# Probability rows of 64 bytes, earlier transposes for the second unit, and the last scatter behind the conditional slots

## The chip, the cores and the metric

The kernel runs on one core of a Trainium2 chip. Its time is the device time of one execution in microseconds. TensorE is called PE here, VectorE DVE, ScalarE ACT, GpSimd Pool, SyncE SP; `SPq` and `POOLq` are instructions of a queue itself (issues of transfers, waits, loads of a register).

## What is computed

Three stages in a row on [4, 576, 512] activations, all in float32. First attention in 8 heads with a causal window of 64. Then a gated feed-forward layer with a convolution of three taps:

```python
h = relu(x @ w_in)
conv = sum(conv_w[k] * hp[:, k:k + S, :] for k in range(3))
y = (h * sigmoid(conv)) @ w_out
```

Then a mixture of 8 experts, in which a token takes its own best expert or holds that of the token before it:

```python
fresh = argmax(logits[b, s])
e = fresh if s == 0 or local_gate[b, s] < 0.5 else prev_e
out[b, s] = p[e] * (relu(y[b, s] @ w1[e]) @ w2[e])     # p = softmax(logits[b, s])
```

## The kernel before

**Layers one and two.** `main(b)` takes the four batches in turn; `attention` of the next batch is woven into the feed-forward products of this one. `ffn_out` (line 478) makes 128 rows of `y` in PSUM with 24 products of 512 columns; ACT moves them into one of two `ysb` buffers (line 499), and SP writes them to `y_dram` (line 500). A row of `y_dram` has 528 columns: 512 of `y` and 16 more, of which column 512 is to hold the token's probability. The last block of 128 rows is made in two halves of 24 products of 256 columns by `ffn_out_last` (lines 503 to 536).

**Routing.** `route_init` (line 729) sets up constants; SP writes zeros into the 16 further columns of `y_dram`, 128 rows at a time (line 789). The gates and the chosen experts follow behind the last batch's products. `chosen` (line 881) ends with the probability of each token in `psel`, 128 partitions x 18, and writes it twice from SP: into `p_dram`, one float for a token (line 888), and into column 512 of `y_dram` (line 889). `slots_of` sorts the tokens by expert into slots and ends with the lists `gidx` (which rows a slot reads, line 992) and `sidx` (which rows it writes), the experts of the slots, and the count of slots `tcnt`.

**Units.** A unit is a slot of 128 tokens of one expert ("S") or a group of two slots and 32 further rows of one expert ("B"). 14 units always run (`NU`): S, then five times B and S, then three S. The rows of a unit are gathered from `y_dram` by Pool (`gather`, line 1146), transposed by PE and split into a high and a low part by ACT and DVE (`X`, line 1168); `take` copies the gathered probability into `pcur`. The first unit is different: most of its rows are gathered before the last block is done (line 1361), those of the last two blocks are added by products with selection matrices within `ffn_out_last` (`x_half`, line 512, after ten products of the second half), and its probabilities are gathered from `p_dram` (line 1366).

`step(t)` (line 1262) is the order of work of one unit, written out by hand: `first_S` or `first_B` makes the hidden layer with the split weights of `w1`, `HT` transposes it, `second_S` or `second_B` multiplies by `w2`. `ahead()` transposes the next unit's rows and starts gathers of later units. `job()` runs a split of weights: a cast on ACT (line 1111) and the remainder on DVE (line 1115). For unit 0, `ahead()` stands behind all 24 products of `second_S`. `second_S` ends with an eviction on ACT that scales by `pcur` (line 1246), and a scatter by Pool to `out` (line 1160). SP loads the weights of later units under a condition (a slot with the same expert needs none).

**Conditional slots.** Behind the 14 units every engine loads the count of slots (line 1420), compares and branches (line 1424). Up to six more slots would run there, each one nested in the condition of the slot before it (`alone`, line 1338); no product of them stands in this trace.

PE, DVE and ACT follow the order of the code (`manual_schedule`); so do Pool and SP in the last stage.

Of the kernel before, what the change touches and what calls it, by code (L numbers as in the profile page):

```python
# [21 lines left out]
def kernel(  # L22
# [14 lines left out]
    nc = tc.nc  # L37
# [20 lines left out]
    dram = ctx.enter_context(tc.tile_pool(name="dram", bufs=1, space=DRAM))  # L58
    DY = DM + 16
    y_dram = dram.tile([N, DY], F32, name="y_dram")  # L60
    p_dram = dram.tile([N, 1], F32, name="p_dram")

    ident = const.tile([P, P], F32, name="ident")
    make_identity(nc, ident)
# [29 lines left out]
    if True:  # L94
# [616 lines left out]
        R0 = 2 * S // P  # L711
        gidx = const.tile([P, NCOL], I32, name="gidx")
        sidx = const.tile([P, NCOL], I32, name="sidx")
        pcur = [const.tile([P, 3], F32, name=f"pcur{i}") for i in range(2)]
        nc.gpsimd.memset(pcur[0], 0.0)
        eslot = const.tile([1, NS + NB], I32, name="eslot")
        tcnt = const.tile([1, 1], I32, name="tcnt")
# [11 lines left out]
        def route_init():  # L729
# [54 lines left out]
            tl("A", [P, NT, P], BF16)  # L784
            tl("aZ", [P, 2, P])
            nc.gpsimd.memset(tl("x0", [P, DY]), 0.0)
            for i in range(NT):
                w = slice(0, DY) if i >= NT - 2 else slice(DM, DY)
                nc.sync.dma_start(out=y_dram[i * P:(i + 1) * P, w], in_=rt["x0"][:, w])
# [91 lines left out]
        def chosen():  # L881

            ex = rt["ex"]
            nc.vector.tensor_tensor(ex, ex, rt["oh"], op=ALU.mult)
            psel = rt["psel"] = r1.tile([P, NT], F32, name="psel")
            nc.vector.tensor_reduce(psel, ex, axis=AX.X, op=ALU.add)
            nc.vector.tensor_tensor(psel, psel, rt["ssum"], op=ALU.mult)
            nc.sync.dma_start(out=p_dram[:, :].rearrange("(i p) o -> p (i o)", p=P), in_=psel)
            nc.sync.dma_start(out=y_dram[:, DM:DM + 1].rearrange("(i p) o -> p (i o)", p=P), in_=psel)

        def slots_of():
# [254 lines left out]
    def gather(t):  # L1146
        for g, (c, _, n) in zip(rows(t), cols(t)):
# [3 lines left out]
                bounds_check=N - 1, oob_is_err=False,  # L1151
            )

    def take(t):

        for j, (g, (_, _, n)) in enumerate(zip(rows(t), cols(t))):
            nc.gpsimd.tensor_copy(pcur[t % 2][0:n, j:j + 1], g[0:n, DM:DM + 1])

    def scatter(c, n, o):
        nc.gpsimd.indirect_dma_start(  # L1160
# [70 lines left out]
            nc.vector.scalar_tensor_tensor(hl[:, f], ps, 0.0, hh[:, f].bitcast(F32), op0=ALU.max, op1=ALU.subtract)  # L1231
            after(f)

    def second_S(t, mids={}):
        hh, hl = (x[:, :, 0:P] for x in hT)
        ps = ps_o.tile([P, DM], F32, tag="o", name="psO")
        n = 0
        for f in range(KF):
            H_, L_ = (w[:, f % 2, :] for w in w2_set[f // 2])
            for a, w in ((hh, H_), (hh, L_), (hl, H_)):  # L1240
                nc.tensor.matmul(ps, a[:, f], w, start=n == 0, stop=n == 3 * KF - 1)  # L1241
                n += 1
                for m in mids.get(n, ()):
                    m()
        c = cols(t)[0][0]
        nc.scalar.activation(o_v[0], ps, AF.Copy, scale=pcur[t % 2][:, 0:1])
        scatter(c, P, o_v[0])

    def second_B(t, after):
        hh, hl = hT  # L1250
# [11 lines left out]
    def step(t, first=(), second=(), late=()):  # L1262

        kind = units[t][0]
        end = t + 1 == NU
        before = t and units[t - 1][0] == "B"
        jobs = list(first)

        def job(n=1):
            for _ in range(n):  # L1270
                if jobs:
                    jobs.pop(0)()

        def ahead():
            if not end:
                X(t + 1)
                n = 4 if t > 2 * NB - 3 else 3
                while coming[0] < min(t + n, NU):
                    gather(coming[0])
                    coming[0] += 1  # L1280

        if kind == "S":
            y = [lambda j=j: Y(t - 1, j) for j in range(3)] if before else [lambda: None] * 3
            job(2)
            first_S(t, {
                (0, 6): (y[0], job), (0, 10): (y[1],),
                (1, 7): (lambda: job(9), lambda: HT(0), *late), (1, 10): (y[2],),
            })
            if t:
                ahead()  # L1290
            jobs.extend(second)
            second_S(t, {3: (lambda: HT(1), lambda: job(9))})
            if not t:
                ahead()
        else:
            first_B(t, lambda f: job())
            job(9)
            ahead()
            jobs.extend(second)
            second_B(t, lambda d: job(2))  # L1300
            job(9)

    def w1_jobs(t):
        if t >= NU:
# [17 lines left out]
    def run():  # L1322
        gather(1)
        load1(1)
        cast(raw2, w2_set, KORD[3])
        for kk in KORD:
            rest_of(raw2, w2_set, kk)
        load2(1)
        for t in range(NU):
            if t == 0:  # L1330
                step(t, (), w1_jobs(1))
            elif units[t][0] == "B":
                step(t, w1_jobs(t + 1) + w2_jobs(t), w1_jobs(t + 2))
            else:
                *w, (c, r) = w2_jobs(t, True)
                step(t, w + [c], w1_jobs(t + 2) if t > 2 * NB - 1 else (), (r,))

    def alone(t):

# [7 lines left out]
        first_S(t)  # L1347
        HT(0)
        HT(1)
        second_S(t)  # L1350

    def tail():
        first = [ffn_out(i, False, 1) for i in (I0, I0 + 1)]
# [5 lines left out]
        for i in range(I0 + 2, NT):  # L1359
            if i == NT - 1:  # L1360
# [3 lines left out]
                    bounds_check=N - 2 * P - 1, oob_is_err=False,  # L1364
                )
                nc.gpsimd.indirect_dma_start(
                    out=pcur[0][:, 0:1], out_offset=None, in_=p_dram[:, :],
                    in_offset=bass.IndirectOffsetOnAxis(ap=gidx[:, 0:1].bitcast(U32), axis=0),
                    bounds_check=N - 1, oob_is_err=False,
                )  # L1370
# [2 lines left out]
    with tc.manual_schedule(engines={mybir.EngineType.PE, mybir.EngineType.DVE, mybir.EngineType.Activation}):  # L1373
# [42 lines left out]
        ps_o = ctx.enter_context(tc.tile_pool(name="ps_o", bufs=2, space=PSUM))  # L1416
        ps_y = ctx.enter_context(tc.tile_pool(name="ps_y", bufs=2, space=PSUM))
        with tc.manual_schedule():
            run()
    slots = nc.values_load(tcnt[0:1, 0:1], min_val=0, max_val=NS)  # L1420

    def others(t):
# [3 lines left out]
                others(t + 1)  # L1426

    others(NU)


# [27 lines left out]
```

## Time and profile before

| | |
|---|---|
| median of 3 runs | 640.96 us (640.54 to 641.39) |
| profiled execution: its time | 641.02 us |
| its span, first to last instruction | 639.0 us |
| mean granted clock of PE | 0.981 of 2.4 GHz |
| busy share of PE, DVE, ACT, Pool | 94%, 66%, 62%, 21% |
| moved by the DMA engines | 92.19 MB, 144 GB/s in the mean |

The profile is one execution. Times in it are microseconds from the start of the span. The chain that ended last is followed back from the last instruction, at each step to what released it. An idle time in brackets stands just before the instruction it belongs to, with what ended it.

### The profile page before, as it was taken

The numbers are of one execution on the slowest core, as the hardware profiler recorded it, in microseconds if no ns is written. First come the engines' busy times: TensorE is split into PE (matmuls) and PEld (weight loads), VectorE is DVE, ScalarE is ACT, GpSimd is POOL, SyncE is SP. The second block draws the span as 40 slices with busy tenths as digits, with TensorE's granted clock in tenths as the row PEclk, the third lists the DMA queues.
The fourth block names the chain that finished last, engine by engine and source line by source line (L and its number), as shares of the span: only waits on it lengthen the run. The fifth ranks groups of instructions, "written<-read, shape, count | busy, mean of one in ns | idle before, by whom it ended". The sixth has DMA issues, their size and how long they took to land.

```text
span 639.0 us, 12841 instructions
## 1 busy us (share of the span) xinstructions
PE 603.3 (94%) x4648; PEld 549.0 (86%) x4648; DVE 420.4 (66%) x972; ACT 394.7 (62%) x926; POOL 134.7 (21%) x198
## 2 busy tenths in 40 slices
PE   6779999999999999999999699999999999999993
PEld 4658998899999999999977688989899899898872
DVE  3888999626883268825868568548556485576860
ACT  3477788646795477934734157657655576567850
POOL 3412000001431023322520122132031320303200
PEclk9889999999999999999999899999999999999997
DMA  7893524442324221118108768858759583433830
GB/s 180 202 244 83 163 66 104 102 122 54 72 61 115 67 54 35 34 36 284 54 1 20 191 226 286 280 185 298 272 174 326 178 269 140 142 91 119 289 135 14
DMA packets 104342, 92.19 MB, mean 144 GB/s; under 512 B 78626, under 2 KB 78898, under 8 KB 104272
## 3 DMA queue, kind: packets, MB, share of 16 engines
q1 hardware_dynamic: 99152, 79.48, 43.5%
q0 software_dynamic: 3488, 10.24, 4.6%
q10 hardware_dynamic: 1632, 1.57, 0.9%
q8 instruction: 39, 0.64, 0.4%
q14 instruction: 31, 0.25, 0.1%
HBM read 89.53 MB, written 10.72 MB: 157 GB/s over the span
## 4 chain that ended last, share of the span: by engine, by line
PE 64%; DVE 12%; DMA 10%; issue 8%; ACT 4%; ACTq 0%; POOLq 0%; POOL 0%; DVEq 0%
PE psO L486 13%; PE psM L444 11%; PE psH L1228 10%; PE psO L1257 8%; PE psO L1241 4%; DMA out_dram<-o,sidx 4%; PE psH L1210 4%; PE psA L221 3%; DMA y_dram<-ysb 2%; DMA raw<-in_moe_w_in_dram 2%; PE psA L298 2%; PE psA L273 1%; DVE lf L572 1%; PE psA L188 1%; DVE lf L574 1%
## 5 line engine op out<-in xcount | busy, mean ns | idle before, releaser
L444 PE MATMUL psM<-x,winH 128*128 128x288 f32 x512 | 109.3, 303 | 0.0
L473 POOL TENSOR_TENSOR gL<-h,gH 128x64 fp32r<-128x64 f32 (+5 forms) x46 | 44.3, 973 | 207.3 <-PE psO L486 121.3
L444 PEld LDWEIGHTS psM<-x,winH 128*128 128x128 f32 x512 | 81.9, 188 | 1.1 <-DVE x L311 0.2
L444 PE MATMUL psM<-x,winL 128*128 128x288 f32 x256 | 75.3, 295 | 0.0
L486 PE MATMUL psO<-woutH,gH 128*128 128x262 f32 (+2 forms) x240 | 68.2, 314 | 1.3 <-ACT gH L472 1.0
L1115 DVE TENSOR_TENSOR x<-raw,x 128x1024 fp32r<-128x1024 f32 x42 | 50.3, 1224 | 27.9 <-ACT x L1111 27.3
L486 PE MATMUL psO<-woutL,gH 128*128 128x262 f32 (+2 forms) x240 | 66.0, 302 | 0.0
L486 PE MATMUL psO<-woutH,gL 128*128 128x262 f32 (+2 forms) x240 | 64.9, 301 | 0.0
L245 ACT ACTIVATE sS<-sS,mx 128x128 f32<-128x128 f32 (+1 forms) x144 | 55.1, 387 | 7.9 <-DVE mx L233 7.9
L1160 POOL DMA_INDIRECT out_dram<-o,sidx x24 | 29.6, 1234 | 141.6 <-ACT o L1196 60.5
L1257 PE MATMUL psO<-gH,x 128*128 128x288 f32 x240 | 51.7, 297 | 0.0
L1228 PE MATMUL psH<-gH,woutH 128*128 128x288 f32 x160 | 48.3, 302 | 0.7 <-ACT gH L1174 0.7
L444 PEld LDWEIGHTS psM<-x,winL 128*128 128x128 f32 x256 | 48.0, 188 | 0.1
L1228 PE MATMUL psH<-gL,woutH 128*128 128x288 f32 x160 | 47.4, 296 | 0.5 <-DVE gL L1175 0.5
L1228 PE MATMUL psH<-gH,woutL 128*128 128x288 f32 x160 | 47.2, 295 | 0.0
L486 PEld LDWEIGHTS psO<-woutH,gH 128*128 128x128 f32 x240 | 42.3, 189 | 4.0 <-ACT gH L472 1.4
L486 PEld LDWEIGHTS psO<-woutL,gH 128*128 128x128 f32 x240 | 42.7, 189 | 1.3
L486 PEld LDWEIGHTS psO<-woutH,gL 128*128 128x128 f32 x240 | 42.3, 189 | 1.1
L1111 ACT ACTIVATE x<-raw 128x1024 fp32r<-128x1024 f32 x42 | 43.0, 1056 | 0.0
L1115 DVE TENSOR_TENSOR woutL<-raw,woutH 128x1024 fp32r<-128x1024 f32 x28 | 32.9, 1223 | 13.6 <-ACT woutH L1111 8.2
L1257 PEld LDWEIGHTS psO<-gH,x 128*128 128x128 f32 x240 | 39.7, 188 | 0.0
L233 DVE CUSTOM_DVE_ANT_0 sS<-psA,mask 128x128 f32<-128x128 f32 (+1 forms) x126 | 28.8, 277 | 13.6 <-PE psA L221 10.5
(380 smaller groups left out, 1596.3 us busy)
## 6 DMA issues: line engine op xcount, KB each, us to landing
raw<-in_moe_w_dram SPq DMA_DIRECT2D x112, 512.0 KB
v<-in_v_dram SPq DMA_DIRECT2D x56, 128.0 KB
y_dram<-ysb SPq DMA_DIRECT2D x17, 256.0 KB
kt<-in_k_dram SPq DMA_DIRECT2D x32, 128.0 KB
raw<-in_moe_w_out_dram SPq DMA_DIRECT2D x8, 512.0 KB
qt<-in_q_dram SPq DMA_DIRECT2D x30, 128.0 KB
raw<-in_moe_w_in_dram SPq DMA_DIRECT2D x6, 512.0 KB
raw<-in_moe_w_in_dram ACTq DMA_DIRECT2D x2, 512.0 KB
```

What stands on the lines that cost most here:

```text
L233: nc.vector.tensor_tensor_reduce(sS[:, c, lo:P], ps[:, j * P + lo:(j + 1) * P], mask[:, lo:P], -scale, -NEG, op0=ALU.add, op1=ALU.min, acc ...
L245: nc.scalar.activation(sS[:, c, lo:P], sS[:, c, lo:P], AF.Exp, scale=-1.0, bias=mx[:, c:c + 1], accum_out=sume[:, c:c + 1],)
L444: nc.tensor.matmul(ps[:, 0:HS], wt[:, kk, f * P:(f + 1) * P], xt[:, c0:c0 + HS], start=n == 0, stop=n == 3 * KD - 1,)
L473: e1.tensor_tensor(gL[:, f, r:r + m], t[:, done:done + m], gH[:, f, r:r + m].bitcast(F32), op=ALU.subtract)
L486: nc.tensor.matmul(p_[:, 0:cs.stop - cs.start], gt[:, kk, r:r + P], wt[:, kk, cs], start=n == 0, stop=n == 3 * KF - 1,)
L1111: nc.scalar.activation(dst[kk][0], raws[kk], AF.Copy)
L1115: nc.vector.tensor_tensor(L_, raws[kk], H_.bitcast(F32), op=ALU.subtract)
L1160: nc.gpsimd.indirect_dma_start(out=out[:, :], out_offset=bass.IndirectOffsetOnAxis(ap=sidx[0:n, c:c + 1].bitcast(U32), axis=0), in_=o[0:n] ...
L1210: nc.tensor.matmul(ps, a, w[:, g * DM:(g + 1) * DM], start=n == 0, stop=n == 3 * KD - 1)
L1228: nc.tensor.matmul(ps, a, w, start=n == 0, stop=n == 3 * KD - 1)
L1241: nc.tensor.matmul(ps, a[:, f], w, start=n == 0, stop=n == 3 * KF - 1)
L1257: nc.tensor.matmul(ps, a, w[:, f], start=n == 0, stop=n == 3 * KF - 1)
```

## The change

`p_dram` gets 16 columns, so that a token's probability has a row of 64 bytes to itself; column 0 holds it. `route_init` writes zeros over all of it from `x0`, ahead of the zeros for `y_dram`. `chosen` writes `psel` into column 0, and the first unit's gather reads rows of 16 floats into `pcur`, which grows from 3 to 16 columns. In unit 0, `ahead()` runs after 18 products of `second_S` and not after 24. The last unit's `second_S` returns its eviction and scatter as a function, which is called behind the conditional slots; these then have a PSUM tile of another pool and another `pcur` (`pair`), so that both last until then.

```diff
--- before.py
+++ after.py
@@ -58,7 +58,7 @@
     dram = ctx.enter_context(tc.tile_pool(name="dram", bufs=1, space=DRAM))
     DY = DM + 16
     y_dram = dram.tile([N, DY], F32, name="y_dram")
-    p_dram = dram.tile([N, 1], F32, name="p_dram")
+    p_dram = dram.tile([N, DY - DM], F32, name="p_dram")
 
     ident = const.tile([P, P], F32, name="ident")
     make_identity(nc, ident)
@@ -711,7 +711,7 @@
         R0 = 2 * S // P
         gidx = const.tile([P, NCOL], I32, name="gidx")
         sidx = const.tile([P, NCOL], I32, name="sidx")
-        pcur = [const.tile([P, 3], F32, name=f"pcur{i}") for i in range(2)]
+        pcur = [const.tile([P, DY - DM], F32, name=f"pcur{i}") for i in range(2)]
         nc.gpsimd.memset(pcur[0], 0.0)
         eslot = const.tile([1, NS + NB], I32, name="eslot")
         tcnt = const.tile([1, 1], I32, name="tcnt")
@@ -784,6 +784,10 @@
             tl("A", [P, NT, P], BF16)
             tl("aZ", [P, 2, P])
             nc.gpsimd.memset(tl("x0", [P, DY]), 0.0)
+            nc.sync.dma_start(
+                out=p_dram[:, :].rearrange("(i p) o -> p i o", p=P),
+                in_=rt["x0"][:, 0:NT * (DY - DM)].rearrange("p (i o) -> p i o", i=NT),
+            )
             for i in range(NT):
                 w = slice(0, DY) if i >= NT - 2 else slice(DM, DY)
                 nc.sync.dma_start(out=y_dram[i * P:(i + 1) * P, w], in_=rt["x0"][:, w])
@@ -885,7 +889,7 @@
             psel = rt["psel"] = r1.tile([P, NT], F32, name="psel")
             nc.vector.tensor_reduce(psel, ex, axis=AX.X, op=ALU.add)
             nc.vector.tensor_tensor(psel, psel, rt["ssum"], op=ALU.mult)
-            nc.sync.dma_start(out=p_dram[:, :].rearrange("(i p) o -> p (i o)", p=P), in_=psel)
+            nc.sync.dma_start(out=p_dram[:, 0:1].rearrange("(i p) o -> p (i o)", p=P), in_=psel)
             nc.sync.dma_start(out=y_dram[:, DM:DM + 1].rearrange("(i p) o -> p (i o)", p=P), in_=psel)
 
         def slots_of():
@@ -1151,10 +1155,14 @@
                 bounds_check=N - 1, oob_is_err=False,
             )
 
+    def pair(t):
+
+        return t % 2 if t < NU else NU % 2
+
     def take(t):
 
         for j, (g, (_, _, n)) in enumerate(zip(rows(t), cols(t))):
-            nc.gpsimd.tensor_copy(pcur[t % 2][0:n, j:j + 1], g[0:n, DM:DM + 1])
+            nc.gpsimd.tensor_copy(pcur[pair(t)][0:n, j:j + 1], g[0:n, DM:DM + 1])
 
     def scatter(c, n, o):
         nc.gpsimd.indirect_dma_start(
@@ -1231,9 +1239,10 @@
             nc.vector.scalar_tensor_tensor(hl[:, f], ps, 0.0, hh[:, f].bitcast(F32), op0=ALU.max, op1=ALU.subtract)
             after(f)
 
-    def second_S(t, mids={}):
+    def second_S(t, mids={}, ps=None):
         hh, hl = (x[:, :, 0:P] for x in hT)
-        ps = ps_o.tile([P, DM], F32, tag="o", name="psO")
+        if ps is None:
+            ps = ps_o.tile([P, DM], F32, tag="o", name="psO")
         n = 0
         for f in range(KF):
             H_, L_ = (w[:, f % 2, :] for w in w2_set[f // 2])
@@ -1242,9 +1251,14 @@
                 n += 1
                 for m in mids.get(n, ()):
                     m()
-        c = cols(t)[0][0]
-        nc.scalar.activation(o_v[0], ps, AF.Copy, scale=pcur[t % 2][:, 0:1])
-        scatter(c, P, o_v[0])
+
+        def last():
+            nc.scalar.activation(o_v[0], ps, AF.Copy, scale=pcur[pair(t)][:, 0:1])
+            scatter(cols(t)[0][0], P, o_v[0])
+
+        if t + 1 == NU:
+            return last
+        last()
 
     def second_B(t, after):
         hh, hl = hT
@@ -1289,16 +1303,15 @@
             if t:
                 ahead()
             jobs.extend(second)
-            second_S(t, {3: (lambda: HT(1), lambda: job(9))})
-            if not t:
-                ahead()
+            left = second_S(t, {3: (lambda: HT(1), lambda: job(9)), 18: () if t else (ahead,)})
         else:
             first_B(t, lambda f: job())
             job(9)
             ahead()
             jobs.extend(second)
-            second_B(t, lambda d: job(2))
+            left = second_B(t, lambda d: job(2))
             job(9)
+        return left
 
     def w1_jobs(t):
         if t >= NU:
@@ -1327,13 +1340,15 @@
             rest_of(raw2, w2_set, kk)
         load2(1)
         for t in range(NU):
+            left = None
             if t == 0:
                 step(t, (), w1_jobs(1))
             elif units[t][0] == "B":
                 step(t, w1_jobs(t + 1) + w2_jobs(t), w1_jobs(t + 2))
             else:
                 *w, (c, r) = w2_jobs(t, True)
-                step(t, w + [c], w1_jobs(t + 2) if t > 2 * NB - 1 else (), (r,))
+                left = step(t, w + [c], w1_jobs(t + 2) if t > 2 * NB - 1 else (), (r,))
+        return left
 
     def alone(t):
 
@@ -1347,7 +1362,7 @@
         first_S(t)
         HT(0)
         HT(1)
-        second_S(t)
+        second_S(t, ps=ps_y.tile([P, DM], F32, tag="y", name="psY"))
 
     def tail():
         first = [ffn_out(i, False, 1) for i in (I0, I0 + 1)]
@@ -1364,7 +1379,7 @@
                     bounds_check=N - 2 * P - 1, oob_is_err=False,
                 )
                 nc.gpsimd.indirect_dma_start(
-                    out=pcur[0][:, 0:1], out_offset=None, in_=p_dram[:, :],
+                    out=pcur[0], out_offset=None, in_=p_dram[:, :],
                     in_offset=bass.IndirectOffsetOnAxis(ap=gidx[:, 0:1].bitcast(U32), axis=0),
                     bounds_check=N - 1, oob_is_err=False,
                 )
@@ -1416,7 +1431,7 @@
         ps_o = ctx.enter_context(tc.tile_pool(name="ps_o", bufs=2, space=PSUM))
         ps_y = ctx.enter_context(tc.tile_pool(name="ps_y", bufs=2, space=PSUM))
         with tc.manual_schedule():
-            run()
+            finish = run()
     slots = nc.values_load(tcnt[0:1, 0:1], min_val=0, max_val=NS)
 
     def others(t):
@@ -1426,6 +1441,7 @@
                 others(t + 1)
 
     others(NU)
+    finish()
 
 
 # ---- launch: one core; inputs and outputs as the reference has them ----
```

## Rows read from the trace of the kernel before

**Rows 1.** The page's slices: busy tenths of PE.

```profile
PE   6779999999999999999999699999999999999993
```

**Rows 2.** Chain that ended last, 300 to 400: start, us, what.

```profile
347.03 11.07 DMA y_dram<-ysb
...
358.98 4.16 DMA x<-y_dram,gidx
```

**Rows 3.** Timeline of PE, 338 to 392: start, us, what, idle before.

```profile
353.45 0.28 PE L526 MATMUL psO<-woutH,gH 128*128 128x256 f32 x1
...
358.50 0.39 PE L526 MATMUL psO<-woutH,gH 128*128 128x256 f32 x1 [2.02 <-ACT ysb L499]
...
363.18 0.80 PE L516 MATMUL psX<-ident,x 128*128 128x128 f32 x2 [3.21 <-DMA x<-y_dram,gidx]
...
368.75 0.39 PE L516 MATMUL psX<-ident,x 128*128 128x128 f32 x2
...
370.30 0.48 PE L1210 MATMUL psH<-winH,x 128*128 128x512 f32 x1
...
385.55 0.40 PE L1228 MATMUL psH<-gL,woutH 128*128 128x288 f32 x1 [0.48 <-DVE gL L1175]
```

**Rows 4.** Timeline of ACT, 338 to 402.

```profile
357.85 0.60 ACT L499 ACTIVATE ysb<-psO 128x512 f32<-128x512 f32 x1 [5.19 <-DMA y_dram<-ysb]
```

**Rows 5.** Stretches: length, busy us by engine, PEclk (granted clock), DMA share, GB/s.

```profile
356.50:360.00 3.50, 1.46 (x10) 1.25 (x10) 3.44 (x5) 0.87 (x2) 1.02 (x1) 1.00 0.25 87
...
363.00:366.00 3.00, 2.82 (x13) 2.82 (x14) 0.00 (x0) 0.00 (x0) 0.00 (x0) 0.50 0.93 352
```

**Rows 6.** Timeline of SP's queue, 338 to 402.

```profile
340.39 0.37 SPq L888 DMA_DIRECT2D p_dram<-psel  x1
340.98 0.93 SPq L889 DMA_DIRECT2D y_dram<-psel  x1
```

**Rows 7.** DMA engines, 338 to 361, 40 slices of 0.575 us: busy tenths, GB/s.

```profile
DMA  0000757799379778999999999778989720000980
GB/s 0 0 0 0 292 165 7 7 5 1 1 1 2 1 1 1 1 1 1 1 5 8 19 25 21 39 43 103 150 146 203 100 68 14 0 0 0 367 317 0
```

**Rows 8.** Line 500's instructions: duration ns min/median/max, first and last start.

```profile
L500 SPq DMA_DIRECT2D y_dram<-ysb x17: 319/339/5016, 124.8 to 358.5; - x17
```

**Rows 9.** Timeline of the last microseconds.

```profile
628.25 0.69 ACT L1246 ACTIVATE o<-psO,pcur 128x512 f32<-128x512 f32 x1 [4.44 <-PE psO L1241]
629.21 0.97 POOL L1160 DMA_INDIRECT out_dram<-o,sidx  x1 [11.41 <-ACT o L1246]
```

**Rows 10.** Timeline of VectorE (DVE), 338 to 402.

```profile
353.43 0.18 DVE L992 TENSOR_SCALAR gidx<-psR 128x30 int32<-128x30 f32 x1
...
355.02 4.63 DVE L1115 TENSOR_TENSOR winL<-raw,winH 128x1024 fp32r<-128x1024 f32 x4
...
379.46 4.63 DVE L1115 TENSOR_TENSOR woutL<-raw,woutH 128x1024 fp32r<-128x1024 f32 x4 [0.26 <-ACT woutH L1111]
```

**Rows 11.** Line 789's instructions (columns as in rows 8).

```profile
L789 SPq DMA_DIRECT2D y_dram<-x x18: 319/430/742, 285.6 to 306.4; - x18
```

**Rows 12.** SP's waits, 280 to 380: us in total, times, longest.

```profile
SPq L500 <- ACT ysb L499: 37.7, 2, 32.8
```

**Rows 13.** Line 1424's instructions, the conditional block.

```profile
L1424 POOLq EVENT_SEMAPHORE  x5: 17/43/2454, 629.8 to 632.5; - x5
...
L1424 PEldq COMPARE_BRANCH  x1: 3456/3456/3456, 625.2 to 625.2; - x1
...
L1424 POOLq INC_SWDGE_SEM  x1: 1240/1240/1240, 632.6 to 632.6; - x1
```

**Rows 14.** Line 1454's instructions, the program's end.

```profile
L1454 SPq EVENT_SEMAPHORE  x14: 17/28/28, 633.8 to 639.0; - x14
...
L1454 POOLq DRAIN  x3: 46/103/4321, 633.9 to 638.8; - x3
L1454 SPq DRAIN  x3: 7/7/13, 634.5 to 638.5; - x3
```

## What the change will do: the prediction

> **What bounds the kernel now.** I began with the page's slices: those of TensorE (PE) stand at 9, but for the first few, one in the middle and the last [rows 1]. A change that takes no product away can gain only where PE stands still, so the next view was the chain that ended last, around that slice. There the chain leaves PE: a dump of 128 rows of `y` into `y_dram` takes 11.07 us to land, and then the gather of the first unit's rows, which reads that buffer, takes 4.16 us [rows 2]. PE's own timeline shows what this costs: the 24 products of the last row block's first half start at 353.45 and PE falls idle at 358.50 - 2.02 = 356.48 (less the last one's 0.28 us, 23 steps of 0.12 us). It waits 2.02 us for an eviction, does ten products, and waits 3.21 us for the gathered rows [rows 3]. That eviction, ScalarE's (ACT), waited itself until 357.85 for an older dump to leave its buffer [rows 4]. The granted clock fell in that pause: 1.00 until 360, 0.50 of 2.4 GHz (1.2 GHz) in 363 to 366, although PE was at work again [rows 5].
>
> Why does a dump take 11 us? The queue of SP names what stands ahead of it: two writes of `psel`, one into `p_dram` (issued at 340.39) and one into `y_dram` (340.98) [rows 6]. Each is 128 x 18 single elements of 4 bytes, 9.2 KB in all. The rates of the DMA engines in slices of 0.575 us tell how they went: 7, 7 and 5 GB/s from 341.4 to 343.2, which is 10.9 KB, so the whole first list and a little of the second; then 1 GB/s until 349.5 while the engines count as busy; and only then larger packets [rows 7]. One GB/s is about 270 such packets per us. I read it so: a limited number of writes may be on their way, and from 343.2 on the second list goes out only as fast as the first list lands. The first list's 2304 writes then need about 8.5 us from there (until about 351.7, 10.3 us in all). The second list, with the first 256 KB dump behind it, is through by 357.8, when the eviction is released that waits for that dump [rows 4]; that is at most 6 us for as many packets of the same size. The lists differ in one thing: neighbours of the first lie 4 bytes apart, those of the second 2112 bytes. And SP was held 5.016 us in one issue behind them, its longest of 17 [rows 8].
>
> The last place where PE has ended and the clock still runs is the tail: the last eviction starts at 628.25, its scatter at 629.21, and the span ends at 639.0 [rows 9].
>
> **The change, part by part.**
>
> *Rows of 64 bytes.* The 2304 writes of the first list stay, but each goes to a row of its own. Their price is not in the trace; the bounds are 8.5 to 10.3 us (as now) and 0 to 6 us (as the second list). I take the second list's, about 4.5 us, because then both lists are the same kind of write: 4 bytes into a row that no other write of the list touches. Both have landed by 341.4 + 9 = 350.4, at the latest 341.4 + 12 = 353.4. The dumps behind them then land in about 2 us, and nothing waits for them. What is late next? The gather needs its indices `gidx`, written at 353.43 to 353.61 [rows 10]. The scatter of the tail starts 0.27 us after the eviction it waits for (628.25 + 0.69 to 629.21) [rows 9], so I put the gather at 353.9. With 4.16 us to landing [rows 2] PE gets its rows at 358.05 instead of 363.18. Without the first stall PE reaches that point at 353.45 + 34 x 0.12 = 357.5. It waits 0.6 us; 5.1 us are gained.
>
> The clock adds to this. From 363.18 to 368.75 PE does 12 small products and 14 of the half block [rows 3] in 5.57 us. The next 12 small ones, at full clock, take 370.30 - 368.75 = 1.55 us, and 14 x 0.12 is 1.7 us: 3.2 us. A pause of 2.02 us left the clock at 1.00 [rows 5], so one of 0.6 should. Gain 2.4 us; front together **7.5 us**. If both lists need all of 12 us, the gather starts at about 354.3 with the 0.9 us that the Pool engine took from the release to its start (358.10 to 358.98 [rows 2]), PE waits till 358.5, and 7.1 are left. The unit behind it follows: its weights' casts, its transposes and the next gather hang on PE or on each other, and VectorE's splits of the first unit's weights end at 355.02 + 4.63 = 359.65 [rows 10], before their first use at 370.30 - 7.5 = 362.8.
>
> The Trainium skill (DMA: Bandwidth & Descriptors, Specifications) says that transfers under 512 bytes pay a read-modify-write. By that rule the pitch is of no account and only the number of packets is, and the front would gain 0; the 8.5 against at most 6 us speak against it, though two lists in one queue don't prove it.
>
> *The zeroing.* SP gets one more write ahead of 18 that start at 285.6 and end at 306.4 [rows 11]: 2304 packets of 64 bytes. Its issue may cost from 0.93 us, as the other list of 2304, to 0.93 + 5.0 if it holds the queue as that did [rows 6, 8]. Behind it on SP stand the loads of the first unit's weights and two dumps; SP then waits 32.8 us for the next eviction [rows 12], which is the cover. I take 0; without that cover it would be 1 to 6 us. The gather of `pcur` reads 64 bytes for 4 in each row; it is needed by the eviction at the first unit's end, behind all of that unit's products: 0.
>
> *The second unit's transposes, six products up.* PE waits 0.48 us for VectorE's low half of the second unit's rows before its second product at 385.55 [rows 3]. VectorE makes that half right after four splits that run 379.46 to 384.09 without a gap [rows 10], and these stand ahead of it in the code as before. Earlier transposes thus wait for VectorE: PE does the six products later and then waits as long. I take 0. Bounds: 0.5 us gained (the stall gone), 1.4 us lost (six products of 512 columns, twice the 0.12 us of 256 each, fall behind a gather that is late). On Pool the gather of the third unit now stands before the first scatter; nobody waits for that scatter until its buffer is written again, two units later.
>
> *The conditional slots ahead of the last scatter.* Nothing of them runs: each engine loads a count, compares and branches, and Pool corrects its semaphores. Pool does that now behind the last scatter: it waits 2.45 us for the landing (till about 632.4), then 1.24 us in the semaphore instruction from 632.6 [rows 13], then a drain of 4.32 us from 633.9 [rows 14]; 638.2 to 639.0 is the engines' last meeting. After the change the first wait and the 1.24 us lie before the last scatter, where Pool sat idle 11.41 us [rows 9]. ACT's load and branch lie in its idle 4.44 us; even at the 3.456 us that PE's branch took [rows 13] they fit. Should the last eviction wait for PE's branch (625.2 + 3.46 = 628.7) instead of PE's last product, it costs 0.5. Then only the drain follows the scatter. Its price there is not known: nearly nothing (0.05 to 0.1, Pool's other two drains), if the 4.32 belongs to the semaphore instruction; or 4.32 from the scatter's end at 630.18; or 4.32 from the landing. The first leaves SP's list of waits as the end: 632.4 + 0.8 + 0.8 = 634.0, gain 5.0. The second ends at 634.5 + 0.8 = 635.3, **gain 3.7**. The third ends at 637.5, gain 1.5. I take the middle one: the drain stands behind the work of its own engine, and in the present trace the landing was over before it began.
>
> **Sum.** 641.02 (the profiled execution: span 639.0 and 2.0 around it, and 0.06 above the median of the runs) - 7.5 - 3.7 = **629.8 us**.
>
> **Rivals.**
> *The count of packets sets the backlog, not the pitch.* For it: the engines are busy at 1 GB/s through both lists. Against it: the second list's shorter time. Then the front stays, and the tail alone gives 641.0 - 3.7 = 637.3. The rule of the Trainium skill named above (DMA: Bandwidth & Descriptors, Specifications) would make this the case.
> *The tail gives nothing or 1.5,* because the drain follows the landing or the last eviction waits for branches: 632 to 633.5.
> *The new pitch is worse* (the other side): one partition's 18 writes now step 128 rows of 64 bytes, 8 KiB, against 512 bytes before. If such steps land more slowly, the whole front moves with the list, one to one, for PE stands idle already. If the list takes twice its 10.3 us, the time is 641.0 + 10.3 - 3.7 = 647.6. It decides from 5 us more on (3.7 of the tail plus the bound of a measurement). For it there is no row; the second list's steps are wider still, and it went faster.
> *Neither part does what it may:* 641.
>
> **Chances.** Both parts work: 0.60, with a range of its own of 628.3 to 632.2 (drain short; clock not regained). Count, not pitch: 0.19. Front alone: 0.08. Worse pitch: 0.07. Nothing: 0.06. About 0.2%, 1.3 us, is what a measurement of this kernel can tell from no change. Faster is 0.60 + 0.19 + 0.08 = 0.87, the same 0.06, slower 0.07. The range 627.8 to 638.0 holds the first three but for some tenth of them, 0.8.
>
> **What would show it.** Front: the slices of 1 GB/s between 343 and 350 gone or short; SP's longest issue there well under 5 us; the gather's start at about 354, set by `gidx`; PE's wait before its products about 0.6 us and the granted clock 1.00 right through. Tail: the semaphore instruction of 1.24 us ahead of the last scatter, the drain beginning right behind it; span from the last eviction's start to the end about 7.1 us instead of 10.8. The second unit's first products should still wait for VectorE. The prediction is wrong if the dumps still take 11 us, or if the drain moves with the landing.

## The result and the profile after

The changed kernel takes 631.48 us in the median of 4 runs (630.25 to 632.09), the one before 641.17 (640.54 to 641.57) in runs beside them: a ratio of 0.9847 [0.9828, 0.9866], 9.7 us faster. The profiled execution is the fastest of the four, 630.25 us with a span of 628.1 (before 641.02 and 639.0). The median lies 1.7 us above the forecast of 629.8, inside the range and inside the likeliest case's own range. The profile, read line by line below, is therefore 1.2 us faster than the median.

The slices of the page, which answer to [rows 1], and the granted clock:

```profile
PE   6778999999999999999999999999999999999995
PEclk9799999999999999999999999999999999999998
```

The dent in the middle of PE's slices is gone, and so is the dip of the clock that went with it. Before, the clock's slices were:

```profile
PEclk9889999999999999999999899999999999999997
```

Windows of the pause and of the products behind it say the same (columns as in [rows 5]):

```profile
356.50:360.00 3.50, 3.38 (x29) 3.18 (x28) 3.50 (x4) 0.39 (x1) 1.74 (x1) 1.00 0.72 218
363.00:366.00 3.00, 3.00 (x17) 2.62 (x18) 1.46 (x2) 1.33 (x2) 0.00 (x0) 1.00 0.95 352
```

The DMA engines in 40 slices of 0.575 us from 338 to 361, against [rows 7]:

```profile
DMA  1000003957769998643850000000001075960999
GB/s 28 0 0 0 0 0 121 331 8 7 7 5 6 56 86 125 46 53 50 303 182 14 0 0 0 0 0 0 0 0 28 0 292 157 235 243 18 306 344 408
```

Five slices of 5 to 8 GB/s carry some 19 KB, as much as both lists; then the dumps go at 46 to 303 GB/s. No slice stands at 1. SP's issues of dumps are held no longer than 1.787 us, where one took 5.016 [rows 8], and the issue of the new zeros is short:

```profile
L500 SPq DMA_DIRECT2D y_dram<-ysb x17: 320/339/1787, 126.0 to 355.7; - x17
```

```profile
L787 SPq DMA_DIRECT2D p_dram<-x x1: 371/371/371, 286.9 to 286.9; - x1
```

The chain of waits no longer passes through a dump there, but through VectorE's index and the gather it releases, which is what the prediction named as next. Further on it passes through the dump of the last half block and the gather of the second unit:

```profile
354.87 0.10 DVE gidx L996
354.97 0.29 DVE ge L999 x2
355.26 3.86 DMA x<-y_dram,gidx
...
362.91 4.97 DMA y_dram<-ysb
...
368.66 6.97 DMA gH<-y_dram,gidx
```

PE's timeline at the places of [rows 3]. No bracket, that is no idle time long enough to be shown, stands at the first product that needs the gathered rows:

```profile
354.82 0.28 PE L526 MATMUL psO<-woutH,gH 128*128 128x256 f32 x1
...
359.16 0.49 PE L516 MATMUL psX<-ident,x 128*128 128x128 f32 x2
...
362.29 0.39 PE L516 MATMUL psX<-ident,x 128*128 128x128 f32 x2
...
375.76 0.63 PE L1181 MATMUL psX<-ident,gH 128*128 128x128 f32 x4 [0.90 <-DMA gH<-y_dram,gidx]
...
379.09 0.40 PE L1236 MATMUL psH<-gL,woutH 128*128 128x288 f32 x1
```

The tail's timeline, against [rows 9]:

```profile
621.00 0.69 ACT L1256 ACTIVATE o<-psO,pcur 128x512 f32<-128x512 f32 x1 [4.40 <-PE psO L1250]
621.96 0.97 POOL L1168 DMA_INDIRECT out_dram<-o,sidx  x1 [11.36 <-ACT o L1256]
```

The conditional block (line 1439 now), against [rows 13]:

```profile
L1439 POOLq EVENT_SEMAPHORE  x5: 17/43/1453, 610.2 to 611.9; - x5
L1439 POOLq INC_SWDGE_SEM  x1: 1220/1220/1220, 612.0 to 612.0; - x1
...
L1439 PEldq COMPARE_BRANCH  x1: 3536/3536/3536, 618.0 to 618.0; - x1
```

And the end (line 1470), against [rows 14]:

```profile
L1470 SPq EVENT_SEMAPHORE  x14: 17/28/11426, 613.2 to 628.0; - x14
...
L1470 POOLq DRAIN  x3: 46/109/5536, 621.7 to 627.8; - x3
```

Pool's wait and its semaphore instruction are over by 613.2, ahead of the scatter. The long drain starts at 621.7, before the scatter does, and lasts to 627.27; that is 4.33 us after the scatter's end at 622.93. SP's long wait, which is for the scatter's landing, ends earlier, at 613.2 + 11.4 = 624.6. The drain thus ends 2.7 us behind the landing, where before it ended 5.8 behind it (638.2 and 632.4, [rows 13, 14]): the landing doesn't set the end. PE's branch took 3.5 us and was no obstacle: the eviction started at 621.00, before the branch was through at 621.55.

The two profiled executions, stretch by stretch (us, each stretch ending where the row says; before from [rows 3, 9]):

| stretch ends with | before | after | gained | forecast |
|---|---|---|---|---|
| first product of the half block | 353.45 | 354.82 | -1.37 | 0 |
| first product on the gathered rows | 363.18 | 359.16 | 5.39 | 5.1 |
| first of the next 12 small products | 368.75 | 362.29 | 2.44 | 2.4 |
| second unit's second product | 385.55 | 379.09 | 0.00 | 0 |
| last eviction | 628.25 | 621.00 | 0.79 | 0 |
| end of the span | 639.0 | 628.1 | 3.65 | 3.7 |

The sum is 10.9, the difference of the spans. Two lines were not forecast, -1.37 and 0.79; experiments 2 and 12 bear on them.

### The profile page after: what moved, and what is told of

It reads as the page before. It is cut to its first block, busy times and chain, and to the rows that moved or that the text cites. A ratio compares the mean times of both kernels' runs of the same rounds, so it can differ in the third digit from the quotient of the medians.

```text
span 628.1 us, 12845 instructions
## 1 busy us (share of the span) xinstructions
PE 600.2 (96%) x4648; PEld 546.0 (87%) x4648; DVE 420.6 (67%) x972; ACT 395.1 (63%) x926; POOL 135.2 (22%) x198
## 4 chain that ended last, share of the span: by engine, by line
PE 64%; DVE 14%; DMA 12%; issue 5%; ACT 4%; POOLq 0%; ACTq 0%; POOL 0%; DVEq 0%
PE psO L486 13%; PE psM L444 11%; PE psH L1236 10%; PE psO L1271 8%; DMA out_dram<-o,sidx 6%; PE psO L1250 4%; PE psH L1218 4%; PE psA L221 3%; PE psA L298 2%; DMA raw<-in_moe_w_in_dram 2%; DVE lf L572 1%; PE psA L273 1%; DVE lf L574 1%; PE psA L188 1%; DVE sS L258 1%
```

## The experiments

Experiments 1 to 4 shared one chip (before: 643.19, 640.84 to 644.91, 23 runs), 5 to 7 and 10 another (642.62, 641.79 to 644.28, 13 runs), 8, 9 and 11 a third (641.84, 640.46 to 647.4, 7 runs); 12 ran on the second chip again, with its own runs of the kernel before (643.69, 641.26 to 644.67, 12 runs).

**1. Rows of 64 bytes and their zeroing alone.** `p_dram` and `pcur` of 16 columns, the zeros, `psel` into column 0, the gather of whole rows:

```diff
-    p_dram = dram.tile([N, 1], F32, name="p_dram")
+    p_dram = dram.tile([N, DY - DM], F32, name="p_dram")
...
-            nc.sync.dma_start(out=p_dram[:, :].rearrange("(i p) o -> p (i o)", p=P), in_=psel)
+            nc.sync.dma_start(out=p_dram[:, 0:1].rearrange("(i p) o -> p (i o)", p=P), in_=psel)
```

> Only the probability rows of 64 bytes, with their zeroing. Theory (the pitch of 4 bytes makes the first list slow): the stalls of 2.0 and 3.2 us and the stretch at half clock go, 641.0 - 7.5 to 7.9 = 633.1 to 633.5. If the 1.4 us that the changed kernel's profile loses in its first 60 us belongs to this part, 634.6. Rival (the number of 4-byte packets makes it, not their pitch): 641.

632.87 us (631.96 to 633.53, 5 runs), a ratio of 0.9838 [0.9823, 0.9854]. The transfers, slices as above:

```profile
GB/s 0 28 0 0 0 0 363 95 7 7 6 4 22 41 97 68 39 57 142 164 128 82 39 39 0 0 0 0 0 28 0 171 267 121 279 88 223 308 395 292
```

With the same 2304 packets of 4 bytes in each list, the stretch of 1 GB/s is gone, and the front's gain is there. The pitch (the distance from one float's place to the next one's) sets the backlog, not the count. A wider pitch also spreads the list over more of DRAM, 147 KB in place of 9.2; no run separates the two. The gain, 10.3 us, is larger than the 7.5 read from the one profile: 0.8 of it belongs to the wider `pcur` (experiment 12), and the profiles of experiments 2 and 3, on the same chip, show PE held longer by the old list, for 7.7 and 7.1 us in its two waits where it was 5.2.

**2. The conditional slots alone.** `last()`, `pair` and the other PSUM tile, on the kernel before:

```diff
-            run()
+            finish = run()
...
     others(NU)
+    finish()
```

> Only the conditional slots ahead of the last scatter. Theory (Pool's drain of 4.3 us follows the end of its own last instruction, and the wait for the landing and the semaphore instruction leave the tail): 641.0 - 3.7 = 637.3, front unchanged. Rival (the drain follows the landing): 641.0 - 1.5 = 639.5. Rival (the last eviction waits for PE's branch): 0.5 more than either.

640.69 us (637.42 to 646.55, 12 runs), 0.9965 [0.9943, 0.9988]: 2.3 us by the ratio, 0.8 to 3.7 by its interval, and so the forecast 3.7 lies at its edge. The packed list may be the cause of the spread: in this profile it held PE's half block for 6 us, and not for 2 [rows 3]. The tail itself has the new form: the eviction starts at 631.25, 7.15 us before the end of the span of 638.4; in the profile of experiment 3, which has the old tail, it is 10.80. The stall, then the drain:

```profile
362.83 0.58 PE L526 MATMUL psO<-woutH,gH 128*128 128x256 f32 x1 [6.04 <-ACT ysb L499]
```

```profile
L1468 POOLq DRAIN  x3: 46/109/5568, 632.0 to 638.1; - x3
```

This run also has the late arrival of the first line of the table, though nothing of the change stands ahead of its tail: at 59 us PE waits once for VectorE. The changed kernel waits there too, and the kernel before didn't in its profile:

```profile
59.26 0.53 PE L444 MATMUL psM<-x,winH 128*128 128x288 f32 x2 [1.09 <-DVE x L311]
```

```profile
60.12 0.53 PE L444 MATMUL psM<-x,winH 128*128 128x288 f32 x2 [1.19 <-DVE x L311]
```

**3. The transposes alone.** On the kernel before:

```diff
-            second_S(t, {3: (lambda: HT(1), lambda: job(9))})
-            if not t:
-                ahead()
+            second_S(t, {3: (lambda: HT(1), lambda: job(9)), 18: () if t else (ahead,)})
```

> Only the second unit's transposes, six products up. Theory (VectorE's four splits stand ahead of the second unit's low half and end no earlier): 641.0, the second unit's second product as far behind the second transposes of the first unit's hidden layer as before. Rival (the transposes had set the start): 640.5 or less. Rival (PE waits for the second unit's gather in front of six products and loses them): up to 642.4.

643.99 us (12 runs), 1.0005 [0.9991, 1.0019]: nothing.

**4. Rows and slots, without the move.** The whole change with

```diff
-            left = second_S(t, {3: (lambda: HT(1), lambda: job(9)), 18: () if t else (ahead,)})
+            left = second_S(t, {3: (lambda: HT(1), lambda: job(9))})
+            if not t:
+                ahead()
```

> The whole change without the earlier transposes. Theory (they are worth nothing, as VectorE sets the start): the time of the whole change, 631.0 to 631.5. Rival (PE's wait of 0.9 us for the gather, which the changed kernel has in front of its last six products, costs time): 0.5 to 0.9 less. Rival (the earlier transposes carry part of the gain): 0.5 to 1.2 more.

629.65 us (628.29 to 631.07, 5 runs), 0.9792 [0.9774, 0.981]. PE's timeline shows what the move changes:

```profile
357.64 0.49 PE L516 MATMUL psX<-ident,x 128*128 128x128 f32 x2 [0.18 <-DMA x<-y_dram,gidx]
...
376.70 0.40 PE L1236 MATMUL psH<-gH,woutH 128*128 128x288 f32 x1 [0.49 <-ACT gH L1182]
377.57 0.40 PE L1236 MATMUL psH<-gL,woutH 128*128 128x288 f32 x1 [0.46 <-DVE gL L1183]
```

Here PE waits 0.49 and 0.46 us behind the transposes; with the move it waits 0.90 for the gather ahead of them, and none behind. From the first product on the gathered rows to the second unit's second product both take 19.93 us (377.57 - 357.64, and 379.09 - 359.16).

**5. The whole change again,** with no edit.

> The whole change again, on the chip of the next kernels. Against the kernel before on the same chip: the two parts add up, 7.9 or more in front (more where the kernel before stalls longer) and 3.7 in the tail. Theory (the earlier transposes are worth nothing): within 0.6 us of the change without them. Rival (they cost what PE waits for the gather in front of six products): 0.5 to 1.0 us slower than the change without them.

630.24 us (629.11 to 631.36, 5 runs), 0.9805 [0.9786, 0.9824]. The interval overlaps with that of experiment 4; the two ratios differ by 0.8 us, so the totals don't exclude that the move costs as much. In this profile Pool's last drain ends 4.63 us behind the scatter's end at 622.73, and the end comes 7.4 us after the last eviction's start:

```profile
L1470 POOLq DRAIN  x3: 46/109/5832, 621.5 to 627.9; - x3
```

**6. Version 4 (the kernel of experiment 4) with VectorE's last split of the second unit's weights put behind that unit's rows.**

```diff
-                step(t, (), w1_jobs(1))
+                step(t, (), w1_jobs(1)[:-1] + [lambda: cast(raw1, w1_sets[1], KORD[-1])],
+                     rest=lambda: (rest_of(raw1, w1_sets[1], KORD[-1]), load1(2)))
```

> Rows and slots of the change, the transposes where they were, and VectorE's fourth split of the second unit's weights behind the second unit's low half. Theory (VectorE's four splits set the second unit's start): its second product comes 0.4 to 0.8 us sooner after the first unit's end than in the change without the earlier transposes; the time 0.4 to 0.8 us below it, at the edge of what can be measured. Rival (the gather's landing sets it): no sooner.

629.46 us (628.35 to 629.69, 5 runs), 0.979 [0.9775, 0.9805]: the fastest median on its chip, but not apart from the whole change. The second unit's second product comes 19.86 us behind the first product on the gathered rows, where experiment 4 has 19.93; that is 0.07 us sooner and not the 0.4 to 0.8 of the theory. VectorE is no longer late, but ACT's high half is:

```profile
376.58 1.29 DVE L1183 TENSOR_TENSOR gL<-psX,gH 128x512 fp32r<-128x512 f32 x2 [1.01 <-ACT gH L1182]
```

**7. Version 4 with rows of 16 bytes,** and **8. with rows of 8 bytes.** With 4 columns, and with 2 (`pcur` then has 3) in the same way:

```diff
-    p_dram = dram.tile([N, DY - DM], F32, name="p_dram")
+    p_dram = dram.tile([N, 4], F32, name="p_dram")
...
-        pcur = [const.tile([P, DY - DM], F32, name=f"pcur{i}") for i in range(2)]
+        pcur = [const.tile([P, 4], F32, name=f"pcur{i}") for i in range(2)]
```

> Rows and slots of the change, with probability rows of 16 bytes, so that four of them lie in 64 bytes. Theory a (the writes of one list that share 64 bytes hold each other up, in proportion to their number): the first list takes about a quarter of its 10 us, the dumps land before the gather's indices are there, and the time is that of rows of 64 bytes, 629.7 to 631. Theory b (any sharing of 64 bytes is as slow as all of it): the backlog as before, 641 - 3.7 = 637 or more. Rival (the count of packets): the backlog would have stayed with rows of 64 bytes too.

> As the run with rows of 16 bytes, with rows of 8 bytes: eight writes of the first list in 64 bytes. Theory a (in proportion to how many share 64 bytes): the first list takes about half of its 10 us, both lists land by about 350, the time stays at 629.7 to 631. Theory b (a step: close neighbours are slow as such): the backlog of the kernel before, dumps landing past 355, 637 or more.

630.44 us (629.1 to 635.65, 4 runs), 0.9831 [0.9789, 0.9873], and 631.05 (629.07 to 634.86, 4 runs), 0.9841 [0.9772, 0.9909]. The transfers with 16 bytes, then with 8:

```profile
GB/s 0 0 0 0 68 381 11 7 7 3 3 3 11 44 25 32 121 107 71 93 189 150 75 0 0 0 0 0 28 0 256 200 198 272 0 262 228 433 299 114
```

```profile
GB/s 0 0 0 303 154 7 7 4 2 1 2 1 1 0 1 37 26 4 28 68 210 139 178 139 68 21 0 28 64 363 25 143 279 137 30 274 363 389 356 385
```

With 16 bytes three slices stand at 3 GB/s, with 8 seven at 0 to 2, with 4 eleven at 1 or 2 [rows 7]. The shorter the step, the longer the lists, as theory a of both runs has it. At 8 bytes PE already gets its buffer in time, and the totals, with intervals of 5 to 9 us, don't part from those of 64 bytes.

**9. Only one list.** Version 4, without the write into `p_dram`, so that the first unit's rows come out as zeros:

```diff
-            nc.sync.dma_start(out=p_dram[:, 0:1].rearrange("(i p) o -> p (i o)", p=P), in_=psel)
```

> Rows and slots of the change, the transposes where they were, and the write of the probabilities into their own buffer left out (the first unit's rows come out as zeros); the list into the buffer of y stays. It measures that list by itself. Theory (packets of 4 bytes in rows of their own pass at 7 GB/s, and the dumps follow at once): one list of 9.2 KB is gone in about 1.3 us; the time is that of the change without the earlier transposes, as nothing waits for either list there. Rival (that list is slow by itself too): a stretch of 1 GB/s remains.

One execution, 630.1 us. Of the list into `y_dram`, 9.2 KB, two slices of 6 and 7 GB/s carry 7.5, so by itself it takes some 1.4 us; the dump follows:

```profile
GB/s 28 0 0 0 0 0 189 267 6 7 196 167 53 36 7 0 0 0 0 345 111 0 0 0 0 0 0 0 0 0 28 0 356 140 217 213 49 309 326 435
```

**10. The kernel before, with the packed list in ACT's queue.** 

```diff
-            nc.sync.dma_start(out=p_dram[:, :].rearrange("(i p) o -> p (i o)", p=P), in_=psel)
+            nc.scalar.dma_start(out=p_dram[:, :].rearrange("(i p) o -> p (i o)", p=P), in_=psel)
```

> The kernel before, with only the write of the probabilities into their own buffer issued from ScalarE's queue and not from SP's, rows of 4 bytes as before. Theory (the slow writes hold the 16 engines or what lies behind them, not the queue): the dumps still land late, 641 to 643, as the kernel before. Rival (they hold the queue that they stand in): the dumps pass them, 633 to 634.

644.74 us (643.65 to 646.5, 8 runs), 1.003 [1.0016, 1.0044]: slower. SP's dumps land late all the same, and ACT's eviction waits for one; PE now waits behind ACT already in the routing (timelines of ACT and of PE):

```profile
360.07 0.60 ACT L499 ACTIVATE ysb<-psO 128x512 f32<-128x512 f32 x1 [16.85 <-DMA y_dram<-ysb]
```

```profile
361.82 0.20 PE L989 MATMUL psR<-perm,tab 50*128 50x25 bf16 x1 [7.34 <-ACT tab L927]
```

So it isn't the order in SP's queue alone that holds the dumps: they are late as well when the packed list stands in another queue.

**11. Version 4 with a plain write in place of the last scatter.** It goes to the first 128 rows of the output, so the last unit's rows are left out.

```diff
-            scatter(cols(t)[0][0], P, o_v[0])
+            if t + 1 == NU:
+                nc.sync.dma_start(out=out[0:P, :], in_=o_v[0])
+            else:
+                scatter(cols(t)[0][0], P, o_v[0])
```

> Rows and slots of the change, the transposes where they were; the last unit's scatter by Pool is replaced by a plain write from SP to the first 128 rows of the output, so the last unit's rows are left out. Theory (in the changed kernel's tail Pool's drain, 4.3 us behind the end of its scatter, is what ends last): Pool's drain lies far ahead of the end, and from the last eviction's start to the span's end it takes 0.7 + 0.3 + about 2.2 for the landing + 0.8 + 0.8 = 4.8 us in place of 7.1: 2.3 us less than the change without the earlier transposes, 627.5 to 628. Rival (the end follows the landing, whoever writes): no gain.

628.75 us (627.04 to 629.32, 4 runs), 0.978 [0.9723, 0.9837]; the interval is too wide to tell it from version 4. The profiled run, 629.12, lost some 1.5 us elsewhere: behind the second unit's two waits, 0.68 and 0.51 us, the granted clock fell, and 15 steps of PE took 3.51 us that take 1.98 at full clock (experiment 12 has the same):

```profile
379.50:383.00 3.50, 3.50 (x17) 3.50 (x16) 1.57 (x2) 1.35 (x2) 0.01 (x1) 0.51 0.87 332
```

The tail tells more (its timeline, then the end's line):

```profile
621.86 0.69 ACT L1256 ACTIVATE o<-psO,pcur 128x512 f32<-128x512 f32 x1 [4.41 <-PE psO L1250]
622.57 0.36 SPq L1258 DMA_DIRECT2D out_dram<-o  x1
```

```profile
L1475 POOLq DRAIN  x3: 46/103/4239, 614.1 to 626.9; - x3
```

Pool has nothing to do here behind the conditional block. Its drain of 4.24 us starts at 614.1 and is over at 618.4, while PE still works. The end then comes 627.2 - 621.86 = 5.3 us after the eviction's start, where it was 7.1: 1.8 us sooner, of 2.3 expected. Here SP's wait of 2.2 us for the write's landing is the last long one. The drain goes with Pool's own last work, whatever that is, and not with the landing of the last transfer.

**12. The kernel before with wider `pcur`.** 

```diff
-        pcur = [const.tile([P, 3], F32, name=f"pcur{i}") for i in range(2)]
+        pcur = [const.tile([P, DY - DM], F32, name=f"pcur{i}") for i in range(2)]
```

> The kernel before with nothing changed but the width of the two pcur tiles, 16 columns for 3; the first unit still gathers one column. The stretch from the second unit's second product to the last eviction has shown two lengths so far: 242.7 us with pcur of 3 or 4 columns (the kernel before, the slots change alone, the transposes alone, rows of 16 and of 8 bytes), 241.9 with 16 columns (rows of 64 bytes alone, the whole change, rows of 64 bytes without the move, the run without the first list). Theory A, the width of pcur, which shifts all tiles that stand behind it in SBUF, sets it: 241.9 here, the group of products with the low half of w2 in the B units at 292 ns and not 297, and a time 0.8 us under the kernel before. Theory B, it comes with what the rows of 64 bytes do in the DMA queues or in DRAM: 242.7 and 297 ns here. In both the two stalls in the front stay, and the time is within 1.5 us of the kernel before.

643.68 us (641.22 to 650.93, 10 runs), 0.9996 [0.998, 1.0012]; 0.8 us can't be seen in such totals. The group of products with the low half of `w2` in the B units can (busy time, mean ns): before, with the wider tile, and in the changed kernel:

```profile
L1257 PE MATMUL psO<-gL,x 128*128 128x288 f32 x120 | 35.6, 297 | 0.0
```

```profile
L1257 PE MATMUL psO<-gL,x 128*128 128x288 f32 x120 | 35.0, 292 | 0.0
```

```profile
L1271 PE MATMUL psO<-gL,x 128*128 128x288 f32 x120 | 35.0, 292 | 0.0
```

The width of `pcur` alone moves the group from 297 to 292 ns; in all 14 profiles the 292 goes with 16 columns and the 297 with 3 or 4. The stretch to the last eviction was not shorter here (631.98 - 388.51 = 243.5 us), but for another reason. Behind the second unit's two waits the granted clock fell, as the window of those products and two rows of PE's timeline show:

```profile
388.50:392.50 4.00, 3.99 (x18) 3.99 (x19) 0.46 (x1) 1.29 (x2) 1.06 (x1) 0.57 0.94 347
```

```profile
388.89 0.36 PE L1228 MATMUL psH<-gH,woutH 128*128 128x288 f32 x1
...
392.40 0.31 PE L1228 MATMUL psH<-gH,woutH 128*128 128x288 f32 x1
```

The 15 steps between them took 3.51 us, where the changed kernel does one in 0.13, so 1.98: 1.5 us lost. Without it the stretch is estimated at 241.9, theory A's figure. So the 0.79 us of the table go with the width; 0.6 of them (35.6 - 35.0) are seen in this group.

## Why the prediction came out right

**The pitch of the first list: right.** The choice of the second list's price over the present one is confirmed by experiment 1, and the rival that the count decides is refuted by it. The rule of the Trainium skill (DMA: Bandwidth & Descriptors, Specifications) that transfers under 512 bytes pay a read-modify-write doesn't separate the two kernels: all lists here are of 4 bytes, and behind the packed one the writes went at 1 GB/s while the others passed at 4 to 8. The rule can't say which, and the measurement decides. The second list gave what the argument needed, a price of the same packets at another pitch. The reading that the second list goes out only as fast as the first one lands fits this, but no view shows the landing of single writes.

**The size of that price: too high.** The prediction took 4.5 us for each list, both landed by 350.4. Both had gone by about 345.5, some 1.5 us each, and one alone took 1.4. The upper bound of 6 us, from 351.7 to 357.8, held little but the dumps: up to 349.5 the slices of [rows 7] already add up to 17.8 KB, nearly both lists. It cost the forecast nothing, since the gather already hung on `gidx`: forecast 353.9, and 355.26 less the 1.37 us by which this execution was late is 353.89.

**The wait and the clock: right.** 5.39 us against 5.1. PE's late 1.37 us leave the wait as it is, since the gather came as late; but the gather landed in 3.86 us and not in 4.16, and so the wait, counted in steps as in the forecast of 0.6 us, is 359.16 - (354.82 + 34 x 0.12) = 0.26 us. As an idle time it is too short for a bracket here; in experiment 4 the bracket reads 0.18. The clock stayed at 1.00, and the 26 products took 362.29 - 359.16 = 3.13 us, against 3.2 forecast and 5.57 before. The reason given for the clock, that a pause of 2.02 us had left it at 1.00, was weak, though: it looked only as far as 360, and in experiments 11 and 12 the clock fell behind two waits of 0.68 and 0.51 us.

**The zeroing: right at nothing.** Its issue took 0.37 us, and SP still waited 31.9 us for the next eviction, where it was 32.8 [rows 12].

**The move: right at nothing, but for the reason given only in part.** Experiments 3 and 4 show no gain without or with the rows. VectorE's low half of the rows again follows four splits without a gap, and is done at 379.03, just ahead of the second product at 379.09:

```profile
373.00 4.63 DVE L1119 TENSOR_TENSOR woutL<-raw,woutH 128x1024 fp32r<-128x1024 f32 x4 [0.26 <-ACT woutH L1115]
377.56 1.28 DVE L1183 TENSOR_TENSOR gL<-psX,gH 128x512 fp32r<-128x512 f32 x2
378.75 0.28 DVE L1183 TENSOR_TENSOR gL<-psY,gH 128x128 fp32r<-128x128 f32 x1
```

But the prediction expected PE to wait for VectorE at the second unit's first products, and no such wait is there. PE gives back the 0.9 us that it saved already ahead of the transposes, to a gather that is late; the prediction had this as its bound for a loss. That the two delays are alike, 0.90 us and 0.49 + 0.46, is luck. Nor is VectorE alone late: with one split less ahead of it, ACT's high half held the start to within 0.07 us (experiment 6).

**The tail: right.** 3.65 us against 3.7, by the middle one of three readings: the drain ends 4.33 us after the scatter's end. The landing is excluded, since the drain ended 5.8 us behind it before and 2.7 after. The branch of PE cost nothing, which was the value taken.

**What was not foreseen:** 1.37 us lost ahead of the change, of which 1.19 are one wait at 60 us. It stood in the profiles of experiments 2 and 3, which have the old code up to the tail or up to the second unit, and not in those of experiments 4, 8 and 12, so it comes and goes without the change. What sets it is open. Nor were the 0.79 us foreseen that a tile's width gained in the units (experiment 12). Part of the closeness of 629.8 is therefore luck: two terms that it lacked have opposite signs.

## What to carry to other kernels

When small transfers hold a queue, compare two lists of the same packets in the same trace before blaming their number: here floats in rows of their own took 1.5 us a list, where packed ones held what stood behind them for over 6. Look for the last engine to finish, not only the last product: a drain that follows one engine's own last instruction can be started early by moving that engine's bookkeeping ahead. Moving work up in one engine's order gains nothing as long as what that work waits for, here a gather and another engine's split, is late by the same amount.

## What the runs showed of the hardware

- **Single floats and their distance.** Behind a list of 2304 writes of 4 bytes whose places in DRAM lie 4 bytes apart, the queue's writes go at 1 or 2 GB/s for 11 slices (6.3 us) in the profile before, and for longer in other profiles of the same list, which fits a gain between 9.7 and 12.4 us from chip to chip. At 8 bytes there are seven such slices (4.0 us), at 16 three of 3 GB/s (1.7 us), at 64 and at 2112 bytes none below 4. Whether the distance counts or the piece of DRAM that the list covers wasn't tried.
- **Such writes hold more than their queue.** With the packed list in ACT's queue, SP's dumps waited all the same (experiment 10).
- **Pool's last drain** ended 4.27 to 4.36 us behind the end of Pool's last instruction, were that a scatter or the semaphore instruction, and 4.63 behind it in the profile of experiment 5.
- **PE's branch** took 3.46 to 3.76 us, where ACT's, SP's, Pool's and VectorE's took 45 to 72 ns. In every profile it began 2.8 to 2.9 us ahead of the end of PE's last product and ended behind it, as here from 618.0 to 621.55; how much of it is a wait for those products isn't shown.
- **A small tile's width** changed the mean of 120 products that don't read it by 5 ns (experiment 12). That it shifts the tiles behind it is a guess; where they lie wasn't looked at.
- **The clock** fell to 0.51 and 0.57 in the windows behind two short waits of PE, 0.68 and 0.51 us (experiments 11 and 12), and to 0.51 behind 0.49 and 0.35 in experiment 10. It stayed at 1.00 behind 0.49 and 0.46 in experiment 4, but also behind 0.69 and 0.48 at the same place in the kernel before, so the length of these waits doesn't decide it alone. The move takes these two waits away; whether it also guards against such a fall in some executions wasn't tried.
